# Attention products of two heads at once, in full float32, in the two column halves of TensorE

## The chip, the core and the metric

The program runs on one core of one Trainium2 chip. The metric is the device time of one execution in microseconds (us). The kernel before takes 950.82 us, the median of three runs (950.68 to 951.13). A core has a matrix engine (TensorE; PE in the rows, PEld its weight loads), VectorE (DVE), ScalarE (ACT), GpSimd (POOL), and a queue that issues transfers (SyncE; SPq). Matrix results land in eight PSUM banks. Data enters and leaves by DMA.

## The reference

Four batches of eight heads, 576 positions, head size 64; the result of the attention feeds two dense blocks.

```
scores = q @ k.T / 8 ; bias[i, j] = -(cum[i] - cum[j]), cum = cumsum(max(s, 0))
scores = where(causal, -1e9, scores + min(bias, 0))
attn   = exp(scores - rowmax) / (rowsum + 1e-9)
x      = (attn @ v)  as (2304, 512)          # the attention product of this document
x      = ((x @ w1) * (x @ w2)) @ w3 @ w_out  # 512 -> 1024 -> 1024 -> 512
h      = x @ w_in ; out = (h - tanh(h)) @ w_out2   # 512 -> 2048 -> 512
```

All inputs and the output are float32.

## The kernel before, in words

Nearly all products are made in a reduced format in three parts: an operand is split into a rounded high part and a low rest, and high x high, high x low and low x high are added up in PSUM. `copy` rounds (ScalarE or VectorE), `sub` forms the rest (VectorE or GpSimd), `split` does both. Full float32 needs no split, but each matmul then runs as two records on TensorE, of two array cycles per column each.

One head (`head`) is worked like this. Queries come in five tiles of 64 or 128 rows. For each tile the scores of all keys up to the diagonal are formed in a bank, the bias rows being part of the contraction; VectorE reads the bank, subtracts and takes the row maximum (L664), ScalarE takes the exponential and the row sum (L670). `flip` transposes the tile on TensorE (L702) into a bank, from which it is copied to SBUF. `pv` multiplies by the values: `pv(0)` for queries 0 to 319 (three key chunks, 320, 192 and 64 columns), `pv(1)` for queries 320 to 575 (five chunks, 3 x 256, 192, 64 columns), both in bank 2. After the odd head of a pair, `inverses` turns the row sums into factors: a transpose (L682), a copy, a DMA to DRAM (r_d) and one back that spreads them over partitions (xr); then the pair's output xf is multiplied (L779) and split into xh and xl, which the products with w1 and w2 (L801, six matmuls per step and 128 channels) read. Each product sums over four pairs of heads, so none ends before the fourth pair of a batch is there.

There are two kinds of head. The eight heads of batch 0 (`full`) use full float32 for scores (L651) and for `pv` (L742, 80 stationary columns: 64 of the values and 16 of padding), from buffer `en`. The other 24 heads split queries and keys (qs, kh, kl, q2; L653 and L654) and, for `pv`, the values (vs, high and low side by side: 128 stationary columns) and the transposed tile (eh, el). L746 multiplies both value halves by eh, L744 the high half by el; the two halves of the bank are then added (a copy to pvt, and L753). q2 holds the low part of the queries and, under it, rows of constants from `fix` that select the bias rows of kl; `constants` brings them by two DMAs. The buffers of odd split heads are in a pool `spl`, which opens only when the pool `nat` of batch 0 (rel, en) is closed, at head 8; `constants(1)` follows that.

While batch 0 runs, w1 and w2 are brought in and converted (`assemble`, L489 to L495, then a split), 16 pieces of 128 x 512.

The order of all instructions is made by a planner in the kernel (`Plan.order`): each operation has a price and a priority, and the planner starts on each engine what is ready, in the order of priority, by its own clock. Where its TensorE would wait before 215 us it inserts small matmuls on `msk` (L548, 128 columns, fillers), which compute nothing that is used. Fillers and order are fixed in the program: on the chip a filler runs whether there is a wait or not, and an instruction that waits holds up those behind it on its engine.

After the attention come w3 @ w_out (L861 to L863), the products with it (L899 to L901) and the second dense block (L938, L959 to L961).

Of the kernel before, what the change touches and what calls it, by code (L numbers as in the profile page):

```python
# [29 lines left out]
VW = D + 16  # L30
# [4 lines left out]
EN = 1024 + 128  # L35
# [288 lines left out]
def tile_kernel(ctx, tc, qk, v, s, w1, w2, w3t, w_out, w_in, w_out2, out):  # L324
# [113 lines left out]
    kh = [p_.buf(f"kh{i}", [P, S], F32R) for i, p_ in enumerate((att, spl))]  # L438
    kl = [p_.buf(f"kl{i}", [P, S], F32R, n=2) for i, p_ in enumerate((att, spl))]
    q2 = [p_.buf(f"q2{i}", [P, S], F32R, n=2) for i, p_ in enumerate((att, spl))]  # L440
    vs = [p_.buf(f"vs{i}", [P, 5, P], F32R, n=2) for i, p_ in enumerate((att, spl))]
# [97 lines left out]
    def constants(i):  # L539
        for a in (D, D + 5):  # L540
            dma(lambda a=a: q2[i].t[a:a + 5].bitcast(F32), lambda: fix.t[D:D + 5], 5 * S * 4, [(fix, 1)], [(q2[i], 1)], PARAM["cst"], issue=830.0)
# [18 lines left out]
    for e in e2[:1] + [en] + e2[1:]:  # L560
        if e is en:
            zero([later(en, 1024, EN, low), later(en, 0, D, low)], [P, D], [en], 30, r=scan)
# [7 lines left out]
    for V in rv:  # L570
        zero([lambda V=V: V.t[:, 5 * D:]], [VW - D], [(V, 1)], 30, r=scan)
    for x in (eh, el):
        zero([later(x, EB + 1024, ETOT, low), later(x, 0, D, low)], [P, D], [x], PARAM["kbp"] - 10, r=scan)
# [10 lines left out]
    for a, n, o, w_, ts in ((0, 2 * NH, 0, 2 * S, [0, 1, 3, 4]), (0, NH, 2 * S, S, [2])):  # L584
        v_ = lambda x, a=a, n=n, o=o, w_=w_: x.t[a:a + n, o:o + w_]
        act(lambda v_=v_: nc.scalar.activation(v_(eh), v_(rel), AF.Copy), w_, [(rel, ts)], [(eh, ts)], PARAM["kbp"])
        sub(lambda v_=v_: v_(el), lambda v_=v_: v_(rel), lambda v_=v_: v_(eh), w_, [(rel, ts), (eh, ts)], [(el, ts)], PARAM["kbp"])
    constants(0)
    for n, x in enumerate((eh, el)):
        dma(lambda n=n, x=x: kb_d.t[:, n, 0:3], lambda x=x: x.t[:NH, :3 * S].bitcast(F32).rearrange("h (t s) -> h t s", s=S), NH * 3 * S * 4, [(x, [0, 1, 2])], [kb_d], PARAM["kbp"] + 100)  # L590
        dma(lambda n=n, x=x: kb_d.t[:, n, 3:5], lambda x=x: x.t[NH:2 * NH, :2 * S].bitcast(F32).rearrange("h (t s) -> h t s", s=S), NH * 2 * S * 4, [(x, [3, 4])], [kb_d], PARAM["kbp"] + 100)
# [9 lines left out]
    def head(h, full, groups=(0, 1)):  # L601
# [6 lines left out]
        e, eb = e2[i % len(e2)], 0 if full else EB  # L608
        qa, qb = (0 if 0 in groups else 320), (S if 1 in groups else 320)
        nv = (qb + P - 1) // P  # L610
        R, RV, Q, Q2, KH, KL, V = rqk[i], rv[i], qs[i], q2[i], kh[i], kl[i], vs[i]
# [5 lines left out]
        else:  # L617
# [6 lines left out]
            P * nv * D * 4, [], [(RV, 0)], pr + PARAM["rv"], issue=520.0)  # L624
        rq, rk = (lambda: R.t[:, 0:S]), (lambda: R.t[:, S:2 * S])
        if not full:
# [6 lines left out]
            split(lambda: V.t[:, :nv, 0:D], (V, 0), lambda: V.t[:, :nv, D:], (V, 1), lambda: RV.t[:, :nv * D].rearrange("p (c d) -> p c d", d=D), nv * D + 100, [RV], p_)  # L633
# [57 lines left out]
        def flip(t):  # L691
# [4 lines left out]
            for js in [list(range(min(4, nch)))] + ([[4]] if nch > 4 else []):  # L696
# [8 lines left out]
                if js == [4]:  # L705
                    n, nq = 1, P - D
                    view = lambda d: d.t[:D, eb + 1024 + D:eb + 1024 + P]
                    src = lambda bk=bk: bk.t[:D, D:P]
                else:
                    o = q0 if t < 3 else eb + q0 - 320  # L710
# [6 lines left out]
                if full:  # L717
                    copy(lambda view=view: view(en), src, n * nq, [bk], [(en, [t] if t < 3 else [[0, 1, 3], [2, 4]][t - 3])], p_, psum=True)
                else:
                    split(lambda view=view: view(eh), (eh, t), lambda view=view: view(el), (el, t), src, n * nq, [bk], p_, psum=True)  # L720

        def pv(grp):
            p_ = pr + PARAM["pv"]
            bk = pv_ring.next()
            if grp == 0:
                q0, n, parts = 0, 320, [0, 1, 2]
                lst = [(0, 0, 320, P), (1, 384, 192, P), (2, 768, 64, P)]
            else:
                q0, n, parts = 320, 256, [3, 4]
                lst = [(c, eb + c * 256, 256, P) for c in range(3)] + [(3, eb + 832, 192, P), (4, eb + 1088, 64, P)]  # L730
            X = xf[(h // 2) % 2]
            o = (h % 2) * D
            if full:
                seq = [(x, 0) for x in lst]
            else:
                seq = [(x, 0) for x in lst[:-2]] + [(lst[-1], 0), (lst[-1], 1)] + [(x, 1) for x in lst[:-2]] + [(lst[-2], 0), (lst[-2], 1)]

            def mm():
                for j, ((c, a, w_, kk), low) in enumerate(seq):
                    go = dict(start=j == 0, stop=j == len(seq) - 1, skip_group_check=True)  # L740
                    if full:
                        nc.tensor.matmul(bk.t[:VW, n - w_:n], RV.t[:kk, c * D:c * D + VW], en.t[:kk, a:a + w_], **go)  # L742
# [22 lines left out]
        if 0 in groups:  # L765
            pv(0)
# [246 lines left out]
```

## Time and profile before

| what | value |
| --- | --- |
| median of 3 runs | 950.82 us |
| the profiled execution, its own time | 950.12 us |
| its span, first to last instruction | 948.4 us |
| TensorE busy in the span | 936.3 us (99%) |
| VectorE, ScalarE, GpSimd busy | 686.5, 595.1, 416.5 us |
| share of TensorE in the chain that ended last | 95% |

Times inside the profile count from the start of the span. The busy time of TensorE contains the fillers, and the end of a matmul is modelled: how long a run of matmuls takes is read from the start of its first to the start of what follows. The profiled execution is 1.7 us longer than its span.

### The profile page before, as it was taken

Reading aid. Unit: us, or ns where it says so; the run is one execution under the profiler, and the core shown is the slowest. Engines: PE = TensorE matmul, PEld = TensorE weight load, DVE = VectorE, ACT = ScalarE, POOL = GpSimd, SP = SyncE. Lnnn points to the kernel's source line nnn. Section 1 sums busy time; section 2 is a strip of 40 time slices with the busy share of each in tenths; the row PEclk is TensorE's granted clock in tenths of the full one; section 3 lists DMA queues with packets and bytes.
Section 4 is the critical chain, followed back from the end, with each engine's and each line's share of the span. In section 5 each row is a group of like instructions: output and inputs, shape, how many; then the busy total and the mean of one; then the engine's idle time right before and its main releaser. Section 6 shows DMA issues by size and latency. Waiting matters only on the chain.

```text
span 948.4 us, 15455 instructions
## 1 busy us (share of the span) xinstructions
PE 936.3 (99%) x5214; PEld 822.9 (87%) x5214; DVE 686.5 (72%) x1399; ACT 595.1 (63%) x1329; POOL 416.5 (44%) x354
## 2 busy tenths in 40 slices
PE   9997999999999999999999999999999999999998
PEld 7776999999999999899888888888888888888887
DVE  8998888688786569993699669985555556645654
ACT  5887677788888544443545367766555555665565
POOL 3458766545564244323988525442222222222321
PEclk9997999999999999999999999999999999999999
DMA  5664566575542135476798532221020101000010
GB/s 185 202 203 139 171 186 203 149 240 152 153 145 76 54 109 189 164 237 210 230 373 297 206 133 88 79 100 45 1 88 1 45 1 45 22 23 1 1 46 23
DMA packets 64309, 118.97 MB, mean 125 GB/s; under 512 B 6435, under 2 KB 34323, under 8 KB 64230
## 3 DMA queue, kind: packets, MB, share of 16 engines
q1 hardware_dynamic: 64230, 117.99, 38.4%
q8 instruction: 41, 0.67, 0.3%
q14 instruction: 38, 0.31, 0.1%
HBM read 88.81 MB, written 25.46 MB: 120 GB/s over the span
## 4 chain that ended last, share of the span: by engine, by line
PE 95%; DVE 3%; ACT 1%; issue 1%; DMA 0%; POOL 0%; SPq 0%; DVEq 0%
PE bank L801 21%; PE bank L938 21%; PE bank L961 7%; PE bank L959 7%; PE bank L960 7%; PE bank L702 5%; PE bank L901 3%; PE bank L899 3%; PE bank L900 3%; PE bank L744 2%; PE bank L654 2%; PE bank L653 2%; PE bank L746 2%; PE bank L861 2%; PE bank L651 2%; PE bank L863 2%
## 5 line engine op out<-in xcount | busy, mean ns | idle before, releaser
L393 POOL TENSOR_TENSOR gl<-pg,gh 128x512 fp32r<-128x512 f32 (+1 forms) x78 | 99.9, 1280 | 254.5 <-ACT gh L387 247.7
L938 PE MATMUL bank<-x2b,wih 128*128 128x512 f32 (+1 forms) x640 | 182.6, 370 | 0.0
L938 PEld LDWEIGHTS bank<-x2b,wih 128*128 128x128 f32 x640 | 116.9, 188 | 22.1
L938 PE MATMUL bank<-x2b,wil 128*128 128x512 f32 (+1 forms) x320 | 117.9, 369 | 0.0
L949 DVE TENSOR_TENSOR pg<-bank,u 128x512 f32<-128x512 f32 (+1 forms) x80 | 50.4, 630 | 90.4 <-POOL gl L393 86.3
L961 PE MATMUL bank<-voh,gl 128*128 128x512 f32 x288 | 112.9, 392 | 0.0
L959 PE MATMUL bank<-voh,gh 128*128 128x512 f32 x288 | 112.8, 392 | 0.0
L960 PE MATMUL bank<-vol,gh 128*128 128x512 f32 x288 | 112.7, 391 | 0.0
L670 ACT ACTIVATE e<-e,nmx 128x320 f32<-128x320 f32 (+4 forms) x160 | 89.0, 558 | 37.6 <-DVE nmx L664 36.6
L387 ACT ACTIVATE gh<-pg 128x512 fp32r<-128x512 f32 (+1 forms) x80 | 47.0, 588 | 99.2 <-PE bank L960 95.8
L952 DVE TENSOR_TENSOR th<-bank,th 128x512 f32<-128x512 f32 (+1 forms) x80 | 50.7, 634 | 45.9 <-ACT th L948 45.8
L664 DVE CUSTOM_DVE_ANT_0 e<-bank,msk 128x320 f32<-128x320 f32 (+4 forms) x160 | 65.6, 421 | 23.1 <-PE bank L654 14.5
L953 DVE COPY_PREDICATED pg<-mk,th 128x512 f32<-128x512 uint32 (+1 forms) x80 | 78.2, 978 | 2.5 <-ACT mk L951 0.9
L702 PE MATMUL bank<-ident,e 128*128 128x128 f32 (+1 forms) x480 | 75.3, 274 | 0.5 <-DVE el L391 0.5
L495 DVE SCALAR_TENSOR_TENSOR wt<-wraw,wt 128x512 uint32<-128x512 uint32 x72 | 72.5, 1007 | 0.8
L493 DVE SCALAR_TENSOR_TENSOR wt<-wraw,wt 128x512 uint32<-128x512 uint32 x72 | 71.8, 997 | 1.0
L393 POOL TENSOR_TENSOR xl<-cf,xh 128x512 fp32r<-128x512 f32 (+1 forms) x40 | 54.8, 1396 | 34.3 <-DMA cf<-c_d 23.9
L938 PEld LDWEIGHTS bank<-x2b,wil 128*128 128x128 f32 x320 | 60.3, 188 | 10.6
L801 PE MATMUL bank<-xh,w1h 128*128 128x384 f32 x192 | 68.6, 357 | 0.1
L391 DVE TENSOR_TENSOR el<-bank,eh 64x64 fp32r<-64x64 f32 (+2 forms) x144 | 62.6, 458 | 8.3 <-ACT eh L387 7.0
L801 PE MATMUL bank<-xh,w2h 128*128 128x384 f32 x192 | 67.9, 354 | 0.0
L951 ACT ACTIVATE mk<-u,const 128x512 f32<-128x512 f32 (+1 forms) x80 | 54.1, 676 | 18.8 <-DVE pg L953 18.5
(135 smaller groups left out, 2496.1 us busy)
## 6 DMA issues: line engine op xcount, KB each, us to landing
rqk<-qk SPq DMA_DIRECT2D x24, 576.0 KB
wraw<-w_out SPq DMA_DIRECT2D x24, 512.0 KB
c_d<-cst SPq DMA_DIRECT2D x48, 192.0 KB
wraw<-w SPq DMA_DIRECT2D x16, 512.0 KB
wraw<-w3t SPq DMA_DIRECT2D x16, 512.0 KB
wraw<-w_in SPq DMA_DIRECT2D x16, 512.0 KB
cf<-c_d SPq DMA_DIRECT2D x32, 256.0 KB
x_d<-x2s SPq DMA_DIRECT2D x16, 512.0 KB
```

What stands on the lines that cost most here:

```text
L393: o.append(("POOL", c_pool2(n), lambda: nc.gpsimd.tensor_tensor(dst(), a(), b().bitcast(F32), op=ALU.subtract)))
L493: dve(lambda: nc.vector.scalar_tensor_tensor(t_.t, h32(), 0xC0000000, t_.t, op0=ALU.bitwise_and, op1=ALU.bitwise_or), 512, [r_, t_], [t_], ...
L495: dve(lambda: nc.vector.scalar_tensor_tensor(t_.t, l32(), 29, t_.t, op0=ALU.logical_shift_right, op1=ALU.bitwise_or), 512, [r_, t_], [t_], ...
L664: nc.vector.tensor_tensor_reduce(e.t[:nq, EOFF[t] + k0:EOFF[t] + k1], bk.t[:nq, :k1 - k0], bi.t[:nq, bo + k0:bo + k1], -0.125, 3.0e38 if f ...
L670: act(lambda: nc.scalar.activation(et(), et(), AF.Exp, bias=nmx.t[:nq, i, tm:tm + 1], scale=-1.0, accum_out=ssum.t[:nq, pj, t, i:i + 1]), ...
L702: nc.tensor.transpose(bk.t[:rows, n * P:(n + 1) * P], e.t[:, EOFF[t] + c * P:EOFF[t] + c * P + rows], ident.t)
L801: nc.tensor.matmul(bk.t[:, :TB], w_.t[:, k, f * P:(f + 1) * P], x_.t[:, k, o:o + TB], start=k == 0 and i == 0, stop=k == KC - 1 and i == 2)
L938: nc.tensor.matmul(bk.t[:, :w], w_.t[:, k, a], X2.t[:, i, k, :w], start=k == 0 and n == 0, stop=k == KC - 1 and n == 2)
L953: dve(lambda pg=pg, mk=mk, th=th, c_=c_: nc.vector.copy_predicated(c_(pg), c_(mk).bitcast(U32), c_(th)), w, [mk, th], [pg], pr, two=True)
L959: nc.tensor.matmul(bank[n].t, gh.t[:, a], voh[f].t, start=f == 0, stop=False)
L960: nc.tensor.matmul(bank[n].t, gh.t[:, a], vol[f].t, start=False, stop=False)
L961: nc.tensor.matmul(bank[n].t, gl.t[:, a], voh[f].t, start=False, stop=f == NF2 - 1)
```

## The change

All 32 heads now use full float32 in `pv`, and one `pv` serves a pair of heads. `flip` copies the transposed tile of either head into a buffer of its own (en[0], en[1]); when the odd head of the pair is transposed, `pv` issues for each chunk a matmul of the even head into partitions 0 to 63 of the bank and one of the odd head into 64 to 127. The stationary operands are the raw values (64 columns, no padding), so each of the two uses one half of the array's columns. One copy of 128 partitions takes the result to xf. Gone are vs, eh, el, pvt, their splits and the addition L753. The score operands of odd heads (qs, kh, kl, q2) move from `spl` to the pool `att`, open from the start, and `constants` is called for both at the start. The split of the bias rows goes to a buffer kbs. There are four value buffers instead of two. The table of priorities (`PARAM`) is the same. One build option sets the SBUF scratch of dynamic DMAs.

```diff
+def f_pair(n):
+    return 2 * [(112.0, 0.8333 * n + 8.0)]
...
-    rv = [att.buf(f"rv{i}", [P, 4 * D + VW], n=2) for i in range(2)]
-    en = nat.buf("en", [P, EN], n=5)
-    spl = Pool("spl", "right")
-    qs = [p_.buf(f"qs{i}", [P, S], F32R, n=2) for i, p_ in enumerate((att, spl))]
...
-    vs = [p_.buf(f"vs{i}", [P, 5, P], F32R, n=2) for i, p_ in enumerate((att, spl))]
+    rv = [att.buf(f"rv{i}", [P, 5 * D]) for i in range(4)]
+    kbs = nat.buf("kbs", [P, 3 * S], F32R, n=10)
+    qs = [p_.buf(f"qs{i}", [P, S], F32R, n=2) for i, p_ in enumerate((att, att))]
...
-    eh = att.buf("eh", [P, ETOT], F32R, n=5)
-    el = att.buf("el", [P, ETOT], F32R, n=5)
-    pvt = att.buf("pvt", [D, 320])
+    en = [att.buf(f"en{i}", [P, ETOT], n=5) for i in range(2)]
...
-    constants(0)
...
+    for i in range(2):
+        constants(i)
...
-            split(lambda: V.t[:, :nv, 0:D], (V, 0), lambda: V.t[:, :nv, D:], (V, 1), lambda: RV.t[:, :nv * D].rearrange("p (c d) -> p c d", d=D), nv * D + 100, [RV], p_)
...
-                if full:
-                    copy(lambda view=view: view(en), src, n * nq, [bk], [(en, [t] if t < 3 else [[0, 1, 3], [2, 4]][t - 3])], p_, psum=True)
-                else:
-                    split(lambda view=view: view(eh), (eh, t), lambda view=view: view(el), (el, t), src, n * nq, [bk], p_, psum=True)
+                copy(lambda view=view: view(en[i]), src, n * nq, [bk], [(en[i], t)], p_, psum=True)
...
+            V2 = rv[2 * pj:2 * pj + 2]
...
+                for j, (c, a, w_) in enumerate(lst):
+                    for k in range(2):
+                        nc.tensor.matmul(bk.t[k * D:(k + 1) * D, n - w_:n], V2[k].t[:, c * D:(c + 1) * D], en[k].t[:, a:a + w_],
+                                         start=j == 0, stop=j == len(lst) - 1, skip_group_check=True)
+            pe([y for x in lst for y in f_pair(x[2])], mm, V2 + [(en[k], parts) for k in range(2)], [bk], p_)
+            copy(lambda: X.t[:, q0:q0 + n], lambda: bk.t[:, :n], n, [bk], [X], p_, psum=True)
...
-        if 0 in groups:
+        if 0 in groups and i:
             pv(0)
...
             nat.close()
-            pl.op([("X", 0.0, lambda: None)], w=[eh])
-            spl.open()
-            constants(1)
...
+    nc = bacc.Bacc("TRN2", target_bir_lowering=False, num_devices=1, dynamic_dma_scratch_size=1024)
```

The planner makes a new order of it. Three places. First TensorE before, the end of batch 0: `pv(1)` of head 7 (L742, rv1), `pv(0)` of head 8 (L746 and L744, vs0), and the first scores of head 9 (L653, L654 with q21, one of the two q2). A row's end gives the rows and columns of the result, and "x3" a repetition.

```order
L742 MATMUL bank2_60<-en_136,rv1_107 80x256 x3
L742 MATMUL bank2_60<-en_136,rv1_107 80x192
L742 MATMUL bank2_60<-en_136,rv1_107 80x64
L702 MATMUL bank3_61<-ident_78,e0_113 128x128 x3
L746 MATMUL bank2_60<-eh_119,vs0_112 128x320
L746 MATMUL bank2_60<-eh_119,vs0_112 128x64
L744 MATMUL bank2_60<-el_120,vs0_112 64x64
L744 MATMUL bank2_60<-el_120,vs0_112 64x320
L746 MATMUL bank2_60<-eh_119,vs0_112 128x192
L744 MATMUL bank2_60<-el_120,vs0_112 64x192
L653 MATMUL bank1_59<-kh1_989,qs1_988 64x64
L654 MATMUL bank1_59<-kl1_990,q21_991 64x64
```

TensorE with the change, `pv(1)` of heads 6 and 7, and the next product (L782, formerly L801):

```order
L730 MATMUL bank2_60<-en0_124,rv2_108 64x256
L730 MATMUL bank2_60<-en1_125,rv3_109 64x256
L730 MATMUL bank2_60<-en0_124,rv2_108 64x256
L730 MATMUL bank2_60<-en1_125,rv3_109 64x256
L730 MATMUL bank2_60<-en0_124,rv2_108 64x256
L730 MATMUL bank2_60<-en1_125,rv3_109 64x256
L730 MATMUL bank2_60<-en0_124,rv2_108 64x192
L730 MATMUL bank2_60<-en1_125,rv3_109 64x192
L730 MATMUL bank2_60<-en0_124,rv2_108 64x64
L730 MATMUL bank2_60<-en1_125,rv3_109 64x64
L782 MATMUL bank6_64<-xh_89,w1h_94 128x384
```

Each chunk now stands twice, once with the even head's en0 and rv2 and once with the odd head's en1 and rv3, where before one head's chunks followed each other; of the split products none is left.

Second the queue of DMA issues, before, at the same time of the program: the constants of q21 (`fix`) are behind the loads of heads 9 to 11.

```order
L384 DMA rqk0_103<-qk 128x2x320
L384 DMA rv0_106<-v 128x192
L384 DMA kl1_990<-kb_d_68 10x320
L384 DMA q21_991<-fix_102 5x576
L384 DMA rv1_107<-v 128x192
L384 DMA q21_991<-qs1_988 64x320
L384 DMA rqk1_104<-qk 128x2x320
L384 DMA q21_991<-fix_102 5x576
L384 DMA rv1_107<-v 128x192
L384 DMA kl1_990<-kb_d_68 10x320
```

With the change, at the start of the program:

```order
L386 DMA q20_116<-fix_102 5x576
L386 DMA rqk1_104<-rel_139 3x1x576
L386 DMA rqk0_103<-rel_139 2x1x576
L386 DMA kb_d_68<-kbs_140 32x1728
L386 DMA q20_116<-fix_102 5x576
L386 DMA rqk1_104<-rel_139 2x1x576
L386 DMA q21_117<-fix_102 5x576 x2
L386 DMA kb_d_68<-kbs_140 32x1152
L386 DMA wraw1_81<-w2 128x1024
L386 DMA wraw3_105<-w1 128x1024
```

The constants of q21 (here q21_117) have moved from rows 77 and 81 of this queue's order to row 17, ahead of the second weight piece (wraw1).

Third TensorE with the change, at the scores of head 9 (L649 and L650, formerly L653 and L654): the same place of the work as the last rows of before in the first pair. L698 transposes (formerly L702), L546 is a filler (formerly L548), of a load and a matmul each.

```order
L649 MATMUL bank1_59<-kh1_113,qs1_111 64x64
L650 MATMUL bank1_59<-kl1_115,q21_117 64x64
L649 MATMUL bank0_58<-kh1_113,qs1_111 128x192
L650 MATMUL bank0_58<-kl1_115,q21_117 128x192
L698 MATMUL bank5_63<-ident_78,e0_118 128x128 x2
L546 LDWEIGHTS msk_101
L546 MATMUL bank2_60<-msk_101 128x128
L649 MATMUL bank1_59<-kh1_113,qs1_111 128x320
L650 MATMUL bank1_59<-kl1_115,q21_117 128x320
L698 MATMUL bank3_61<-ident_78,e0_118 128x128 x3
L546 LDWEIGHTS msk_101
L546 MATMUL bank2_60<-msk_101 128x128
```

Here fillers stand between scores and transposes. From the fourth `inverses` transpose to the first product that reads the fourth pair there were 2, and there are 131. In the whole program there are 370 fillers, 164 before; the 206 more all stand before that product. In counts of instructions: VectorE 1401 before and 1202 now, ScalarE 1171 and 1109, GpSimd 356 and 325, DMA issues 443 both.

## Rows read from the trace of the kernel before

**Rows 1.** The page, parts 1, 2 and 4: shares, slices of 23.7 us.

```profile
PE 936.3 (99%) x5214; PEld 822.9 (87%) x5214; DVE 686.5 (72%) x1399; ACT 595.1 (63%) x1329; POOL 416.5 (44%) x354
...
PEclk9997999999999999999999999999999999999999
...
PE 95%; DVE 3%; ACT 1%; issue 1%; DMA 0%; POOL 0%; SPq 0%; DVEq 0%
```

**Rows 2.** Busy us: stretch, PE, PEld, DVE, ACT, POOL; then PEclk, DMA share, GB/s.

```profile
200.00:300.00 100.00, 99.54 (x733) 97.74 (x732) 76.70 (x245) 83.68 (x242) 55.67 (x48) 1.00 0.49 146
```

**Rows 3.** The same for stretches of 10 us up to 100.

```profile
0.00:10.00 10.00, 8.94 (x112) 8.25 (x113) 7.88 (x33) 2.16 (x6) 4.47 (x11) 1.00 0.56 158
...
60.00:70.00 10.00, 10.00 (x61) 7.86 (x61) 9.77 (x29) 9.22 (x26) 5.11 (x5) 1.00 0.61 196
...
80.00:90.00 10.00, 4.58 (x21) 3.97 (x22) 9.91 (x18) 5.67 (x16) 9.13 (x10) 0.64 0.46 124
90.00:100.00 10.00, 10.00 (x61) 9.62 (x61) 7.06 (x26) 7.46 (x25) 5.03 (x5) 0.85 0.52 150
```

**Rows 4.** The chain of waits, 0 to 130 us: start, length, what.

```profile
16.55 0.99 PE bank L742 x6
...
21.19 1.75 PE bank L742 x10
...
24.03 0.56 PE bank L548 x10
```

**Rows 5.** TensorE in order of time, 240 to 246 us: two split head groups.

```profile
240.27 0.55 PE L746 MATMUL bank<-eh,vs 128*128 128x256 f32 x4
...
241.27 0.49 PE L702 MATMUL bank<-ident,e 128*128 128x128 f32 x3
...
245.16 0.34 PE L746 MATMUL bank<-eh,vs 128*128 128x320 f32 x2
...
245.74 0.27 PE L702 MATMUL bank<-ident,e 128*64 128x128 f32 x1
```

**Rows 6.** TensorE in order of time, 73 to 89 us.

```profile
73.01 0.27 PE L653 MATMUL bank<-kh,qs 128*64 128x64 f32 x1
...
73.54 0.27 PE L682 MATMUL bank<-ident,ssum 128*10 128x128 f32 x1
...
74.06 0.60 PE L702 MATMUL bank<-ident,e 128*128 128x128 f32 x4
...
79.29 0.50 PE L702 MATMUL bank<-ident,e 128*128 128x128 f32 x3
81.26 0.41 PE L746 MATMUL bank<-eh,vs 128*128 128x320 f32 x2 [1.46 <-DVE eh L388]
...
82.19 0.19 PE L653 MATMUL bank<-kh,qs 128*64 128x64 f32 x1
86.39 0.29 PE L654 MATMUL bank<-kl,q 74*64 74x64 f32 x1 [4.01 <-DMA q<-fix]
...
88.22 0.67 PE L801 MATMUL bank<-xh,w1h 128*128 128x384 f32 x1
```

**Rows 7.** The DMA queue's issues, 80 to 84 us.

```profile
80.37 0.79 SPq L384 DMA_DIRECT2D q<-fix  x1
...
83.00 0.75 SPq L384 DMA_DIRECT2D q<-fix  x1
```

**Rows 8.** GpSimd in order of time, 82 to 87 us.

```profile
82.27 1.72 POOL L779 TENSOR_TENSOR xf<-xf,xr 128x64 f32<-128x64 f32 x2
...
84.95 1.85 POOL L393 TENSOR_TENSOR xl<-xf,xh 128x576 fp32r<-128x576 f32 x1
```

**Rows 9.** VectorE groups by line and form.

```profile
L391 DVE TENSOR_TENSOR el<-bank,eh 128x512 fp32r<-128x512 f32 x48 | 31.9, 682 | 1.9 <-ACT eh L387 1.5
```

**Rows 10.** Weight loads by line and form.

```profile
L746 PEld LDWEIGHTS bank<-eh,vs 128*128 128x128 f32 x192 | 31.1, 189 | 2.2 <-POOL w1l L393 1.7
...
L744 PEld LDWEIGHTS bank<-el,vs 128*64 128x64 f32 x192 | 19.9, 136 | 0.2 <-DVE el L391 0.2
```

More of the change, by code (lines that the diff above doesn't have):

```diff
@@ L559, in tile_kernel @@
     low = slice(D, P)
-    for e in e2[:1] + [en] + e2[1:]:
-        if e is en:
-            zero([later(en, 1024, EN, low), later(en, 0, D, low)], [P, D], [en], 30, r=scan)
+    for e in e2[:1] + [None] + e2[1:]:
+        if e is None:
+            for x in en:
+                zero([later(x, EB + 1024, ETOT, low), later(x, 0, D, low)], [P, D], [x], 30, r=scan)
             zero([lambda: ssum.t], [20], [ssum], -5, 1.0)
@@ L569, in tile_kernel @@
             zero([later(e, EOFF[0], EOFF[0] + D, low)], [D], [(e, 0)], -10 if e is e2[0] else 92, r=scan)
[L570 to L573, printed above, removed]
     zero([lambda: const.t[:, 0:1]], [1], [const], 5.0e4, SQ_B, r=scan)
@@ L607, in head @@
         n_head[0] += 1
-        e, eb = e2[i % len(e2)], 0 if full else EB
+        e = e2[i % len(e2)]
         qa, qb = (0 if 0 in groups else 320), (S if 1 in groups else 320)
         nv = (qb + P - 1) // P
-        R, RV, Q, Q2, KH, KL, V = rqk[i], rv[i], qs[i], q2[i], kh[i], kl[i], vs[i]
+        R, RV, Q, Q2, KH, KL = rqk[i], rv[2 * pj + i], qs[i], q2[i], kh[i], kl[i]
         rows = D if full else P
@@ L726, in pv @@
                 q0, n, parts = 0, 320, [0, 1, 2]
-                lst = [(0, 0, 320, P), (1, 384, 192, P), (2, 768, 64, P)]
+                lst = [(0, 0, 320), (1, 384, 192), (2, 768, 64)]
             else:
                 q0, n, parts = 320, 256, [3, 4]
-                lst = [(c, eb + c * 256, 256, P) for c in range(3)] + [(3, eb + 832, 192, P), (4, eb + 1088, 64, P)]
+                lst = [(c, EB + c * 256, 256) for c in range(3)] + [(3, EB + 832, 192), (4, EB + 1088, 64)]
             X = xf[(h // 2) % 2]
-            o = (h % 2) * D
@@ L733, in pv @@
[L733 to L736, printed above, removed]
-            def mm():
[L739 to L742, printed above, removed]
-                    elif low:
-                        nc.tensor.matmul(bk.t[:D, n - w_:n], V.t[:kk, c, 0:D], el.t[:kk, a:a + w_], **go)
-                    else:
-                        nc.tensor.matmul(bk.t[:, n - w_:n], V.t[:kk, c, :], eh.t[:kk, a:a + w_], **go)
@@ L747, in pv @@
-            if full:
-                pe([y for (x, _) in seq for y in f_mm4(x[2])], mm, [RV, (en, parts if grp == 0 else range(5))], [bk], p_)
-                copy(lambda: X.t[o:o + D, q0:q0 + n], lambda: bk.t[:D, :n], n, [bk], [(X, h % 2)], p_, psum=True)
-            else:
-                pe([y for (x, low) in seq for y in f_mm(x[2], D if low else P)], mm, [V, (eh, parts), (el, parts)], [bk], p_)
-                copy(lambda: pvt.t[:, :n], lambda: bk.t[D:, :n], n + 300, [bk], [pvt], p_, psum=True)
-                dve(lambda: nc.vector.tensor_tensor(X.t[o:o + D, q0:q0 + n], bk.t[:D, :n], pvt.t[:, :n], op=ALU.add), n, [bk, pvt], [(X, h % 2)], p_, extra=150.0)
+            V2 = rv[2 * pj:2 * pj + 2]
@@ L771, in head @@
                 flip(t)
-            pv(1)
+            if i:
+                pv(1)
         if h % 2:
@@ L835, in tile_kernel @@
         if b == B - 1:
-            spl.close()
             att.close()
```

32 lines of the change are left out of this document (15 added, 17 removed).

## The prediction

> **What bounds the kernel now.** I read the page first. TensorE is busy for 936.3 of 948.4 us and carries 95% of the chain that ended last [rows 1]. A busy figure so near the span says little, since fillers count as work, so I went on to the stretches. From 200 to 300 us TensorE is full (99.54 of 100) while VectorE has 76.70 and GpSimd 55.67 [rows 2]; the clock row shows full clock in all slices but one [rows 1]. After about 100 us the time is thus the sum of what TensorE is given, and relieving another engine is worth nothing there. The first 100 us are different: TensorE shares the bound with VectorE and ScalarE (9.77 and 9.22 of 10 us from 60 to 70), and from 80 to 90 us it is busy for 4.58 of 10 only, at a mean granted clock of 0.64, then at 0.85 from 90 to 100 [rows 3]. So I price three things: the TensorE work of the value products, the fillers, and the hole at 80 us.
>
> **The value products.** In batch 0 a head's two runs of L742 take 0.99 and 1.75 us, 2.74 together, the order being tight there [rows 4]; eight heads 21.9 us. In a split head `pv(1)` runs from 240.27 to 241.27 and `pv(0)` from 245.16 to 245.74, each up to the next transpose [rows 5]: 1.58 us, 24 heads 37.9 us. Before, the value products cost 59.8 us.
>
> With the change a pair has the columns of one L742 head twice, once in each half of the array. No row of before shows two column halves at work together; this is the unknown of the case. Bounds: if the halves run fully side by side, a pair costs what one head did, 2.74 us, 16 pairs 43.8 us, a saving of 16.0. If one waits for the other, it costs 5.48 us, 16 pairs 87.7 us, a loss of 27.9. I take them as side by side, since the two halves share no weights and no result rows, but not perfectly. Each full-precision matmul is two records, and the two of one half must follow each other. In program order the first record of a group has no partner yet, nor has the last. That exposes at most one record per group: 320 of the 1152 columns that `pv(0)` streams (two passes over 576), 0.28 us, and 256 of 2048 in `pv(1)`, 0.22 us. So a pair costs 2.74 to 3.24 us. I take 3.1, in the upper half: 49.6 us, a saving of 10.2.
>
> The Trainium skill, "TensorE: Matmul & The Clock Gate", section "Part 3: Packing small matmuls", says that matmuls in different column tiles run at once, each further tile adding about 4 ns. By it a pair is some 2.8 us (an estimate from that page and L742) and the result some 5 us lower than mine; no run here shows it yet.
>
> **The fillers.** There are 206 more. A run of ten takes 0.56 us [rows 4], 56 ns each: 11.5 us. They run whether needed or not. They stand where the order expects TensorE to wait for the softmax and the weight conversion, and the rows support that: in batch 0 the others are nearly full [rows 3] and the change takes little from them there, eight copies of a result to xf. About 9.5 us of value products leave batch 0 (8 heads at 2.74 less 4 pairs at 3.1), and fillers take their place. This is the part of the gain that I expect not to see.
>
> **The hole at 80 us.** TensorE waits 1.46 us for a split (eh, on VectorE) and then 4.01 us for the constants of q2 [rows 6], whose two transfers are issued only at 80.37 and 83.00 us [rows 7], because odd heads' operands cannot exist before `nat` is closed. Behind that wait in TensorE's queue stand the scores of heads 9 and 10 and then all products. 5.5 us are lost by waiting. Granted clocks of 0.64 and 0.85 mean that the lower of the two levels, 1.2 instead of 2.4 GHz, held for 7.2 of the first 10 us and 3.0 of the next, so from about 82.8 to 93.0 us. TensorE works in it from 86.39 on, 6.6 us at half speed, 3.3 us lost. Together 8.8 us.
>
> With the change the constants come in the first 20 us, and eh is gone. What is late next is the fourth pair: its inverses' transpose is at 73.54 us [rows 6], its output is multiplied from 82.27 and the low part xl ends at 84.95 + 1.85 = 86.80 us [rows 8]: 13.3 us after. So even without the constants no product of that pair could have started before 86.80, against 88.22 in the trace [rows 6]. In the new order, between the same two points, TensorE has 131 fillers (7.3 us), one `pv(1)` and one `pv(0)` (3.1 us), the first three score tiles of three heads (1.0 us each, 73.01 to 74.06 less the small transpose in it [rows 6]), six products of 384 steps and 19 transposes of 256 steps (1.0 and 2.1 us at the 0.43 ns that L742 takes per step, 0.99 us for 2,304), 16.5 us in all. That is longer than 13.3, so I expect the pair to be ready when TensorE gets there, with 3 us to spare. TensorE also reaches the transpose some 4 to 5 us earlier: the value products ahead of it shrink by about 9 us, and 77 of the added fillers (4.3 us) stand there. The fillers also keep the engine from standing still. From 0 to 10 us, where it mainly ran fillers, the granted clock was 1.00 [rows 3], so I take the upper level here and count the 3.3 us as won.
>
> A new order brings waits that its planner did not foresee; the old one had 5.5 us of them here. I add 2.0 us, with 0 and 6 as ends.
>
> **What costs and gives nothing.** VectorE loses 144 subtractions like L391 (682 ns for the largest form [rows 9]) and 48 additions L753, and GpSimd 32 splits of values. All but the first heads' lie after 100 us, beside a full TensorE. If TensorE became so short of work there that VectorE set the pace, it would be seen as idle time; at 76.70 of 100 us, falling, this is far off. The copy of a pair's result covers 128 partitions instead of 64, with the same columns. The second weight piece is issued behind eight more transfers, at up to 0.79 us each [rows 7] 6 us later at most; VectorE has softmax to do in that time, and if it falls behind by this, that is the third rival below.
>
> **The sum.** 948.4 - 10.2 + 11.5 - 8.8 + 2.0 = 942.9 us of span. The profiled execution was 1.7 us longer than its span, and 0.7 below the median of the runs: 945 us.
>
> **The rivals.**
> *The halves take turns.* One stream of columns enters the array at a time, and the second half waits. For it: nothing in the trace shows an overlap of two streams, and L742 with 80 of 128 columns is a single stream. Against it: the two use separate columns and partitions. A pair costs 5.48 instead of 3.1 us, 16 pairs 38 us more, and since the order is fixed nothing absorbs it: 983 us. The change turns slower from 3.1 + 5.8/16, about 3.5 us per pair, on: there the gain of 5.8 us is gone.
> *The weight loads come into the open.* A pair has 32 loads of 64 columns. Loads take 136 ns with 64 columns and 189 with 128 [rows 10], so 64 columns occupy some 53 ns of the load path. If half of the 32 cannot hide beside the other half's stream, 16 pairs pay 13.6 us: 959 us; if all, 972. Against it: in before loads hide behind streams (L744 waited 0.2 us in 192 loads).
> The Trainium skill, "TensorE: Matmul & The Clock Gate", in the same section, states that a load overlaps matmuls in flight only where the row group differs, and both halves use all rows. The trace disagrees for one tile after another, and shows nothing for two halves.
> *The hole stays.* The fourth pair, or the softmax of heads 8 and 9, comes later than the order assumes, TensorE stands still behind it, the clock falls again, and the fillers have run all the same. For it: VectorE had 9.91 of 10 us there [rows 3]. Against it: the 3 us to spare, and less work on VectorE. Then the 8.8 us are not won: 952 us, with the small value of unforeseen waits.
>
> **Chances.** My forecast 0.68, with its own range of 937 to 951 us (2.74 to 3.24 us per pair, 0 to 6 us of new waits); turns 0.12; loads 0.08; hole 0.12. The range that leaves out no more than 2 in 10 reaches over the hole and the cheaper half of the loads, 937 to 960 us; the turns are left out. A measurement of this kernel tells some 0.2% (1.9 us) from no change. Faster than 948.9 us: 0.64 of the forecast's 0.68 and 0.03 of the hole, 0.67. Within: 0.04, 0.07 of the hole and 0.01 of the loads, 0.12. Slower than 952.7: the turns 0.12, loads 0.07, hole 0.02, 0.21.
>
> **What would show it.** In the changed profile the start of a run of L730 to the start of what follows gives the price of a pair: 2.7 to 3.2 us for both groups if the halves overlap, 5.5 if they take turns, 3.9 to 4.8 if loads show, and then the weight loads of L730 have waits of their own. The clock row should have no low slice near 90 us, no wait on q2's constants should be left, and the first dense run of products should start 2 to 4 us earlier than 88.22. The filler group should count 370. After 100 us TensorE should be as full as before, with VectorE lower. I am wrong if TensorE has more idle time before 100 us than the 8.8 us that I take away, if a pair costs over 3.5 us, or if the dense part after 330 us, which the change doesn't touch, changes its length.

## The result: 5.5 us slower, most of it lost before 96 us

The changed kernel takes 956.47 us in the median (955.67 to 957.1, four runs), the kernel before 950.98 beside it: a ratio of 1.0056, 95% interval 1.0039 to 1.0074. The forecast was 945.0 and faster. The profiled execution took 956.8 us with a span of 955.1.

### The profile page after: what moved, and what is told of

Its sections match the earlier page's. It is cut to its first block, busy times and chain, and to the rows that moved or that the text cites. A ratio compares the mean times of both kernels' runs of the same rounds, so it can differ in the third digit from the quotient of the medians.

```text
span 955.1 us, 15454 instructions
## 1 busy us (share of the span) xinstructions
PE 942.2 (99%) x5420; PEld 810.9 (85%) x5420; DVE 611.6 (64%) x1200; ACT 568.8 (60%) x1267; POOL 393.4 (41%) x323
## 4 chain that ended last, share of the span: by engine, by line
PE 95%; DVE 3%; ACT 1%; issue 1%; ACTq 0%; DVEq 0%
PE bank L915 21%; PE bank L782 20%; PE bank L938 7%; PE bank L936 7%; PE bank L937 7%; PE bank L698 5%; PE bank L730 5%; PE bank L876 3%; PE bank L877 3%; PE bank L878 3%; PE bank L546 2%; PE bank L647 2%; PE bank L649 2%; PE bank L650 2%; PE bank L838 2%; PE bank L840 2%
## 5 line engine op out<-in xcount | busy, mean ns | idle before, releaser
L936 PE MATMUL bank<-voh,gh 128*128 128x512 f32 x288 | 112.8, 392 | 0.0
L698 PE MATMUL bank<-ident,e 128*128 128x128 f32 (+1 forms) x480 | 77.0, 276 | 1.7 <-ACT e L666 0.9
L389 ACT ACTIVATE en<-bank 64x64 f32<-64x64 f32 (+3 forms) x166 | 64.3, 407 | 16.9 <-PE bank L698 15.2
L491 DVE SCALAR_TENSOR_TENSOR wt<-wraw,wt 128x512 uint32<-128x512 uint32 x72 | 73.1, 1016 | 1.2
L789 DVE TENSOR_TENSOR cst<-bank,asb 128x384 f32<-128x384 f32 x48 | 26.6, 554 | 68.9 <-PE bank L782 52.4
L782 PE MATMUL bank<-xh,w1h 128*128 128x384 f32 x192 | 69.2, 361 | 0.1
L782 PE MATMUL bank<-xh,w2h 128*128 128x384 f32 x192 | 68.3, 356 | 0.0
```

The source lines that it names most:

```text
L389: pl.op([("ACT", c_act(n, psum), lambda: nc.scalar.activation(dst(), src(), AF.Copy)), ("DVE", c_dve(n, not psum), lambda: nc.vector.tenso ...
L491: dve(lambda: nc.vector.scalar_tensor_tensor(t_.t, h32(), 0xC0000000, t_.t, op0=ALU.bitwise_and, op1=ALU.bitwise_or), 512, [r_, t_], [t_], ...
L698: nc.tensor.transpose(bk.t[:rows, n * P:(n + 1) * P], e.t[:, EOFF[t] + c * P:EOFF[t] + c * P + rows], ident.t)
L782: nc.tensor.matmul(bk.t[:, :TB], w_.t[:, k, f * P:(f + 1) * P], x_.t[:, k, o:o + TB], start=k == 0 and i == 0, stop=k == KC - 1 and i == 2)
L936: nc.tensor.matmul(bank[n].t, gh.t[:, a], voh[f].t, start=f == 0, stop=False)
```

## The profile after

The page of the changed kernel, parts 1 and 2, against [rows 1]:

```profile
PE 942.2 (99%) x5420; PEld 810.9 (85%) x5420; DVE 611.6 (64%) x1200; ACT 568.8 (60%) x1267; POOL 393.4 (41%) x323
...
PEclk9999999999999999999999999999999999999999
```

VectorE lost 75 us of work and TensorE gained 6. Busy time of stretches of the changed kernel (PE, PEld, DVE, ACT, POOL; then PEclk), against [rows 2, 3]:

```profile
80.00:90.00 10.00, 7.15 (x87) 6.75 (x86) 7.76 (x18) 5.35 (x19) 5.37 (x6) 0.90 0.54 169
90.00:100.00 10.00, 9.97 (x92) 8.68 (x91) 6.81 (x17) 5.75 (x20) 6.20 (x7) 0.93 0.35 103
...
200.00:300.00 100.00, 99.95 (x742) 90.28 (x741) 43.95 (x175) 79.28 (x236) 47.02 (x38) 1.00 0.46 142
```

The hole at 80 us is shallower and its clock higher (0.90 against 0.64), but no engine is busy for even 8 of its 10 us, where in [rows 3] VectorE had 9.91: the engines wait for one another. TensorE of the changed kernel in order of time, from the last value products of batch 0 to the first product that reads the fourth pair:

```profile
70.39 1.20 PE L730 MATMUL bank<-en,rv 128*64 128x320 f32 x12
71.85 0.66 PE L698 MATMUL bank<-ident,e 128*128 128x128 f32 x4 [0.26 <-ACT e L666]
...
74.28 0.27 PE L678 MATMUL bank<-ident,ssum 128*10 128x128 f32 x1 [1.39 <-DVE ssum L677]
...
75.59 1.96 PE L730 MATMUL bank<-en,rv 128*64 128x256 f32 x20
77.47 0.44 PE L782 MATMUL bank<-xh,w1h 128*128 128x384 f32 x1
...
87.16 0.27 PE L678 MATMUL bank<-ident,ssum 128*6 128x128 f32 x1 [2.85 <-DVE ssum L677]
...
90.22 1.74 PE L730 MATMUL bank<-en,rv 128*64 128x320 f32 x12
...
95.58 0.42 PE L782 MATMUL bank<-xh,w1h 128*128 128x384 f32 x1
```

The wait for q2's constants is gone, as forecast. In its place stand two waits for the reciprocals of the row sums, at the fourth and the fifth `inverses` transpose (L678), and the dense products start at 95.58 us, not 88.22 [rows 6]. From there to the last matmul it is 855.5 us, 856.2 before. So on balance the loss lies before 96 us. It isn't quite all of it: the new order does more ahead of that product (twelve more transposes, and the fifth pair's `pv(0)` for both its heads), so the rest should be shorter by more than 0.7; but from 100 to 200 us TensorE is busy for 98.2 us, where before it had all 100.

Summed over the trace up to that product, each TensorE instruction counted from its start to the next one's, so that a wait counts for the instruction before it, in us (the last two columns are experiments told below, without the addition L676 in the same order and in a new one):

| | before | after | without the addition | new order |
|---|---|---|---|---|
| fillers | 11.64 | 29.18 | 23.88 | 21.71 |
| value products | 22.93 | 14.55 | 14.02 | 13.64 |
| transposes | 16.90 | 18.12 | 17.80 | 16.69 |
| full scores | 25.35 | 26.54 | 26.53 | 26.20 |
| split scores | 6.90 | 2.64 | 4.05 | 3.17 |
| first products | 3.43 | 3.49 | 3.49 | 3.75 |
| sum | 87.16 | 94.51 | 89.78 | 85.16 |

What VectorE did ahead of the two transposes:

```profile
71.83 2.15 DVE L676 TENSOR_SCALAR ssum<-ssum 128x10 f32<-128x10 f32 x1
74.01 0.22 DVE L677 RECIPROCAL ssum<-ssum 128x10 f32<-128x10 f32 x1
...
83.66 3.13 DVE L676 TENSOR_SCALAR ssum<-ssum 128x6 f32<-128x6 f32 x1 [0.34 <-ACT e L666]
86.82 0.19 DVE L677 RECIPROCAL ssum<-ssum 128x6 f32<-128x6 f32 x1
```

L676 adds 1e-9 to ten or six numbers per partition. Undisturbed it takes 0.16 us; here 2.15 and 3.13. GpSimd of the changed kernel in the same time:

```profile
71.53 1.05 POOL L395 TENSOR_TENSOR kl<-rqk,kh 64x320 fp32r<-64x320 f32 x1
72.55 1.39 POOL L395 TENSOR_TENSOR xl<-xf,xh 128x576 fp32r<-128x576 f32 x1
...
83.11 0.93 POOL L395 TENSOR_TENSOR kl<-rqk,kh 64x320 fp32r<-64x320 f32 x1
84.01 0.32 POOL L760 TENSOR_TENSOR xf<-xf,xr 128x64 f32<-128x64 f32 x1
84.28 1.26 POOL L395 TENSOR_TENSOR w2l<-wt,w2h 128x512 fp32r<-128x512 f32 x1
85.50 1.26 POOL L760 TENSOR_TENSOR xf<-xf,xr 128x512 f32<-128x512 f32 x1
...
93.65 1.71 POOL L395 TENSOR_TENSOR xl<-xf,xh 128x576 fp32r<-128x576 f32 x1 [4.21 <-ACT en L389]
```

GpSimd's runs end at 72.55 + 1.39 = 73.94 and 85.50 + 1.26 = 86.76 us; the additions end at 73.98 and 86.79. So the first waited through two GpSimd instructions, the second through four. That is not the rule. Of the twenty additions in this kernel ten took over 0.25 us; all ten started while GpSimd worked, and eight of them ended with the one GpSimd instruction that they met, three of these although GpSimd's next followed at once, as here:

```profile
123.96 1.43 POOL L395 TENSOR_TENSOR kl<-rqk,kh 64x576 fp32r<-64x576 f32 x1 [0.52 <-DVE kh L390]
124.17 1.25 DVE L676 TENSOR_SCALAR ssum<-ssum 128x6 f32<-128x6 f32 x1
125.35 1.00 POOL L760 TENSOR_TENSOR xf<-xf,xr 128x64 f32<-128x64 f32 x2
```

Why the two on the path waited through more stays open. After that ScalarE's queue loses more:

```profile
87.47 0.27 ACT L389 ACTIVATE rinv<-bank 6x128 f32<-6x128 f32 x1 [3.46 <-PE bank L678]
...
92.04 0.44 ACT L389 ACTIVATE xf<-bank 128x320 f32<-128x320 f32 x1 [2.01 <-PE bank L730]
92.49 0.35 ACT L666 ACTIVATE e<-e,nmx 64x64 f32<-64x64 f32 x1
...
92.84 0.67 ACT L389 ACTIVATE xh<-xf 128x576 fp32r<-128x576 f32 x1
```

The fourth pair's output was multiplied by 86.76, but its rounding to xh stands in the order behind the copy of the next pair's result (xf), which waits for `pv(0)` at 90.22 on TensorE, which stands behind the held transpose at 87.16. So xh starts at 92.84 and xl ends at 95.36. TensorE itself shows no wait after 87.16: the fifth pair's `pv(0)`, head 10's scores and transposes and 61 fillers (4.4 us) stand ahead of the products in its order, and it comes to them at 95.58.

## The experiments

Theory A: the addition, held by GpSimd's runs, makes the fourth and fifth transposes late, and the fixed order turns that into the loss. B: VectorE and ScalarE are short of time as such. C: the added fillers hold TensorE up. Each time below is a median, given beside the kernel before, run on the same chip: 951.0 to 951.2 us in all three sets.

**Without the addition, same order.**

```
-dve(lambda: nc.vector.tensor_scalar(sv(), sv(), 1.0e-9, None, op0=ALU.add), n, [], [(ssum, ks)], ...)
+dve(lambda: None, n, [], [(ssum, ks)], ...)
```

> The changed kernel in its own order, but the addition of 1e-9 to the row sums (L676) issues nothing; a sum is at least 1, so that nothing else changes. Theory A (the small addition is held by GpSimd's runs, 2.15 us ahead of the fourth inverses transpose and 3.13 us ahead of the fifth, and the fixed order passes it on to the products at 95.58 us): the fourth L678 comes near 72.3 instead of 74.28 us, the fifth 3 to 5 us earlier than 87.16, the dense products at 91 to 93, 952 to 954 us in all. Theory B (VectorE's and ScalarE's work as such is late, the addition only waits where others would): the reciprocal or the next instruction waits as long, 956 to 957 us. Theory C (the added fillers hold TensorE up): within 1 us of 956.5.

950.96 us, ratio 0.9992 (0.9984 to 1.0001): 5.5 us less than with the addition, somewhat more than expected. TensorE, then VectorE:

```profile
72.72 0.27 PE L678 MATMUL bank<-ident,ssum 128*10 128x128 f32 x1
...
82.88 0.27 PE L678 MATMUL bank<-ident,ssum 128*6 128x128 f32 x1
...
90.84 0.42 PE L782 MATMUL bank<-xh,w1h 128*128 128x384 f32 x1
```

```profile
82.40 0.19 DVE L677 RECIPROCAL ssum<-ssum 128x6 f32<-128x6 f32 x1 [0.33 <-ACT e L666]
82.51 3.34 DVE L488 TENSOR_SCALAR wt<-wt 128x512 f32<-128x512 f32 x1
...
87.50 0.21 DVE L660 CUSTOM_DVE_ANT_0 e<-bank,msk 64x64 f32<-64x64 f32 x1
```

A holds: the transposes come 1.6 and 4.3 us earlier, the products 4.7, and after the products another 1.1 us of the span are gone. The same GpSimd run now holds the next instruction of that kind, a weight conversion (L488, 0.42 us when free), and behind it head 10's scores; that is left over.

**The kernel before without the addition, same order.** The same edit there.

> The kernel before with the same addition issuing nothing, in its own order. Theory A: there the addition ahead of the fourth and the fifth inverses transpose took 0.16 us and only the one at 41.09 us was held, by 0.8 us: 950 to 951 us, no change that can be measured; the gain of the edit belongs to the new order. If the addition is dear everywhere (after 96 us it is held by up to 1.6 us ten times): 945 to 948 us.

949.53 us, ratio 0.9981 (0.9973 to 0.9990): 1.5 us. A small gain, not none, just outside what A expected; the edit is worth 5.5 in the new order and 1.5 in the old.

**Without the last 146 fillers, same order.**

```
-        nc.tensor.matmul(bank[2].t[:, :P], x, x, start=True, stop=True)
+        if n_[0] <= 224: nc.tensor.matmul(bank[2].t[:, :P], x, x, start=True, stop=True)
```

> The changed kernel in its own order, of the 370 fillers only the first 224 (those up to the third inverses transpose); the other 146, 14 us from start to start, issue nothing. Theory A: they stand where TensorE would wait anyway, so TensorE is idle instead, the dense products start within 1.5 us of 95.58, and 955 to 958 us; if the granted clock falls in the idle time as it did at 80 us in the kernel before (0.64), up to 3 us more, 960. Theory C (the fillers are in the way of ready work): 8 to 14 us of them go, the dense products start at 84 to 88, 945 to 950 us.

957.56 us, ratio 1.0063 (1.0049 to 1.0077); the dense products start at 95.49. Taking these 146 out gains nothing, so C is out as far as they go; the first 224 stayed in. TensorE is idle where fillers were, and its clock falls:

```profile
80.00:90.00 10.00, 5.24 (x28) 3.28 (x27) 8.54 (x22) 4.93 (x20) 4.74 (x6) 0.77 0.57 174
```

The lower clock costs time too, so what a filler costs by itself is not shown by this.

**Each pair's value products head by head.**

```
-for j, (c, a, w_) in enumerate(lst):
-    for k in range(2):
+for k in range(2):
+    for j, (c, a, w_) in enumerate(lst):
```

> The changed kernel, each pair's value products issued as all of one head (one column half), then all of the other, in place of one from each in turn. If two halves overlap only because their instructions alternate: a pair costs about 5.4 us instead of 3.1, of which batch 0 hides a part, 985 to 993 us. If alternation is not what makes it (each instruction takes what it takes): a pair stays at 3.1 us and 956 to 957 us.

984.94 us, ratio 1.0355 (1.0338 to 1.0373). TensorE at the fourth pair, to be set against 70.39 and 75.59 above:

```profile
75.33 1.79 PE L730 MATMUL bank<-en,rv 128*64 128x320 f32 x12
77.05 0.66 PE L698 MATMUL bank<-ident,e 128*128 128x128 f32 x4
...
80.53 3.30 PE L730 MATMUL bank<-en,rv 128*64 128x256 f32 x20
```

The same instructions take 4.95 us per pair from start to start over all 16, against 3.10 in turn: 29.6 us, the difference of the times 28.5. Two halves overlap where their instructions alternate; head by head little of it is left (5.48 would be two L742 heads one after the other).

**The odd heads' constants late again.**

```
-for i in range(2):
-    constants(i)
+constants(0)
...
         nat.close()
+        constants(1, [stack["right"]])
```

> The changed kernel with one step undone: the constants of the odd heads' q2 are fetched only once nat is closed, as in the kernel before; the order is made anew. If the early constants are worth what I gave them (8.8 us of hole): 962 to 966 us. Theory A (GpSimd's hold on small VectorE work and the queue behind it decide when the fourth pair is ready, the constants come in time either way or within its shadow): 955 to 959 us, the dense products again between 94 and 98 us.

970.95 us, ratio 1.0211 (1.0191 to 1.0231), but this doesn't price the constants. In the order made anew they are not as late as in the kernel before: their two transfers are issued at 58.35 us, not at 80.37 and 83.00 [rows 7], and TensorE never waits for them.

```profile
58.35 1.50 SPq L386 DMA_DIRECT2D q<-fix  x2
```

This order starts the dense products at 90.8, 4.8 us earlier than the changed kernel, and loses 12.8 us in waits far behind, at w3's products (in total, how many, the longest):

```profile
PE bank L876 <- ACT xh L389: 7.1, 1, 7.1
PE bank L877 <- POOL xl L395: 5.7, 4, 4.1
```

Neither theory foresaw that. What the early constants are worth by themselves stays open.

**Without the addition and without the last 146 fillers, same order.** The two edits together.

> The run without the addition once more (950.96 us, dense products at 90.84, 3.24 us of waits before them), and without the 146 fillers after the third inverses transpose (about 8.2 us at 56 ns). If these fillers are what TensorE spends its saved time on needlessly: dense products at 83 to 87 us, 943 to 947 us in all. If VectorE, ScalarE and GpSimd set the time of the fourth pair and of the softmax of heads 8 to 10: the waits grow by what the fillers took, dense products at 90 to 91.5, 950 to 952 us (up to 3 us more where the granted clock falls).

951.03 us, ratio 0.9997 (0.9984 to 1.0009); dense products at 90.46 against 90.84 with the fillers. So here, too, the time that the value products give back becomes filler or idle time, whichever one chooses. It agrees with this that TensorE is not the bound before 90 us, but it isn't shown: the clock fell with the idle time (0.66), and that costs time as well; `pv(0)` of the fifth pair took 2.83 us there by its row, 1.20 with the fillers:

```profile
80.00:90.00 10.00, 8.18 (x36) 5.02 (x34) 7.14 (x22) 7.04 (x23) 7.32 (x7) 0.66 0.63 171
```

**Without the addition, the order made anew.** The line of the addition is taken out, so that the planner doesn't see it.

> The changed kernel without the addition, the order made anew (332 fillers instead of 370; other queues move with it). Theory A, on what is left of the loss after the addition is gone (a conversion L488 held 3.34 us by GpSimd ahead of head 10's scores at 82.51, and xh of the fourth pair behind that head's exponentials on ScalarE): a new order doesn't know of these holds either, 947 to 952 us. If the added fillers or the old order's place of xh were the rest: 943 to 946 us.

944.98 us, ratio 0.9933 (0.9921 to 0.9946). ScalarE, GpSimd and TensorE at the fourth pair:

```profile
84.56 0.68 ACT L389 ACTIVATE xh<-xf 128x576 fp32r<-128x576 f32 x1
```

```profile
85.31 1.42 POOL L395 TENSOR_TENSOR xl<-xf,xh 128x576 fp32r<-128x576 f32 x1 [3.01 <-ACT xh L389]
```

```profile
85.92 0.55 PE L697 MATMUL bank<-ident,e 128*128 128x128 f32 x3
86.22 0.42 PE L781 MATMUL bank<-xh,w1h 128*128 128x384 f32 x1
```

Here xh stands ahead of the next pair's copy, GpSimd rests from 82.3 to 85.31 while VectorE converts weights unheld, and the dense products start at 86.22. My expectation by A was too timid: the order has no knowledge of holds, but it met few. Which of the moved instructions did it was not tried one by one. That the time meets the forecast of 945.0 is luck: it is another kernel, in another order.

**And the subtractions on VectorE.** The planner's prices are changed besides, so that it gives the splits' subtractions to VectorE: `dsub0` 979.7 to 0, `dsub` 5134.3 to 600, `pool` -71.7 to 300, `spp` 349.6 to 500, `dcopy0` 29.4 to 10, `dother0` 1000 to 300, `act` -76.1 to -40, `fl` 112.8 to 100, `early` 154617 to 200000.

> As the run with the new order and no addition, and the planner's prices are changed so that the splits' subtractions go to VectorE and hardly any to GpSimd (84 GpSimd rows instead of 328, 1423 VectorE rows instead of 1170). Theory A: with GpSimd's runs gone the VectorE instructions that they held take their undisturbed times (L488 0.42 us, L491 0.69), which is more than the 0.4 to 0.7 us that each subtraction adds to VectorE: dense products at 83 to 88 us, 942 to 948 us. Theory B (VectorE's own work is the bound of the first 90 us): the added subtractions, some 20 there, lengthen it by 10 us: dense products at 96 to 102, 955 to 965 us.

943.76 us, ratio 0.9918 (0.9904 to 0.9932), the fastest of all, 0.8% below the kernel before; dense products at 85.60. From 200 to 300 us VectorE has more to do than in the changed kernel (56.20 against 43.95 us), GpSimd a third of what it had, and TensorE is full:

```profile
200.00:300.00 100.00, 100.00 (x739) 91.49 (x736) 56.20 (x185) 76.23 (x225) 16.15 (x14) 1.00 0.40 122
```

**The kernel before without the addition, the order made anew.**

> The kernel before without the addition, the order made anew: what the change itself is worth once neither kernel has the addition and each has its own order, to be set against 944.98 us of the changed kernel so treated. Theory A: in the kernel before the addition cost 1.5 us in its old order, and a new order of this kernel moves no limit: 948 to 952 us; the change is then worth 3 to 7 us. If a new order helps any kernel as much as it helped the changed one (6 us beyond the addition): 942 to 946 us, and the change is worth nothing.

954.84 us, ratio 1.0037 (1.0024 to 1.0051): slower than in its old order (949.53), outside both expectations. Its first dense run starts at 93.28, and the constants' wait is there:

```profile
PE bank L654 <- DMA q<-fix: 2.6, 1, 2.6
```

So making the order anew moves either kernel by 5 to 6 us, the one up and the other down, and a single order doesn't tell the worth of the change.

**The addition with GpSimd quiet, and the same order without it.** The prices of the run at 943.76, once with the addition and once with it issuing nothing.

> The changed kernel with the addition in it, and the subtractions of the splits on VectorE (87 GpSimd rows instead of 325): the order is made anew with those prices. To be compared with the next run, which has the same order without the addition. Theory A (GpSimd's runs hold the addition): with GpSimd nearly silent the additions take 0.15 to 0.3 us, and the two runs differ by less than 1.5 us (in the old order the addition cost 5.5). If the addition is dear by itself: again 4 to 6 us apart.

> As the run before it in the same order, the addition issuing nothing. Theory A: within 1.5 us of it, both at 944 to 950 us (the planner of this order still reserves time for the addition, so that it is not the order of the run at 943.76). If the addition is dear by itself: 4 to 6 us faster than the run before it.

949.97 us (ratio 0.9987, 0.9975 to 0.9998) with it, 950.20 (0.9993, 0.9981 to 1.0005) without. The addition's twenty instances (duration min, median, max in ns), first in the changed kernel, then in the quiet one:

```profile
L676 DVE TENSOR_SCALAR ssum<-ssum x20: 156/222/3130, 24.1 to 300.2; 128x10 f32<-128x10 f32 x12, 128x6 f32<-128x6 f32 x4, 128x4 f32<-128x4 f32 x4
```

```profile
L676 DVE TENSOR_SCALAR ssum<-ssum x20: 153/162/1119, 23.8 to 294.8; 128x10 f32<-128x10 f32 x12, 128x6 f32<-128x6 f32 x4, 128x4 f32<-128x4 f32 x4
```

In this order the addition costs nothing that can be told from the scatter of the runs (948.8 to 952.5 us with it, 948.5 to 953.5 without). The order is a new one as well, so the two times alone don't speak for GpSimd; the durations do: the longest is 1.12 us here, under one of the few GpSimd instructions left, and 3.13 there. Together with the run without the addition and the ends of the held additions this is what A rests on. The order weighs much here, too: the run at 943.76 has the same prices and no addition either, and 950.20 is 6.4 us more.

**The kernel before with the subtractions on VectorE.** The addition taken out, the same prices.

> The kernel before without the addition and with the subtractions on VectorE (1614 VectorE rows instead of 1373, 126 of GpSimd instead of 359): what the same repair does without the change. Theory A: VectorE has 76.70 us of work in each 100 there, and 15 more don't fit beside what it must do in time; TensorE waits for it and the time is 960 to 985 us: the repair is open only because the change takes 144 subtractions and 48 additions from VectorE. If GpSimd's holds are what VectorE suffers from in the kernel before too: 944 to 950 us.

972.97 us, ratio 1.0229 (1.0213 to 1.0245). That is inside A's range, but the trace doesn't show A's mechanism. VectorE has 92 of the first 100 us, yet so it has in the run at 943.76 (92.61), and the first dense run starts at 88.77, only 0.55 later than in the kernel before. The loss lies behind it. TensorE is idle for 13.9 of the 160 us from 340 to 500, where VectorE has 126.94 us of work; the kernel before has 129.28 there:

```profile
340.00:500.00 160.00, 146.08 (x718) 130.39 (x717) 126.94 (x212) 70.64 (x124) 31.35 (x21) 0.95 0.58 185
```

The largest waits are for the rounding of splits, on ScalarE:

```profile
PE bank L800 <- ACT xh L387: 7.6, 2, 4.6
...
PE bank L898 <- ACT xh L387: 6.8, 1, 6.8
```

The second stands at w3's products, as in the run with late constants. The prices were sought for the changed kernel, so this is no best order of the old one. That the repair needs the VectorE time that the change sets free is therefore not shown.

## Why the prediction was wrong

*The value products: right.* 3.1 us per pair and 49.6 us in all were forecast; L730 takes 49.6 from start to start. The rival of halves in turn is out: 3.10 us alternating, 4.95 head by head. So is the rival of open weight loads, which would have shown as 3.9 to 4.8. What makes the 0.36 us over one head's 2.74 was not tried. The estimate of some 2.8 us by the Trainium skill ("TensorE: Matmul & The Clock Gate", "Part 3: Packing small matmuls") was 0.3 too low, and its rule on loads by row groups, in the same section, did not bind here: a pair's 32 loads of 137 ns, 4.4 us in all, went into its 3.10 us.

*The fillers: right in size, wrong as a cost.* 370 run; up to the dense products they take 12.2 us more than before without the addition (11.5 forecast), 17.5 with it, since the waits and low clock behind them are counted there. But taking 146 out moves the dense products by no more than 0.4 us in either order, and saves nothing. I summed them as work where TensorE was not the bound; the sum came out because they fill what the value products leave.

*The hole: here it failed.* With the value products and the fillers as forecast the span would stand at 949.7 us. The hole and the new waits together were to take 6.8 us off it; they put 5.4 on (955.1), and without the addition they take 0.5 off (949.2). Two sentences on the hole were wrong. "TensorE also reaches the transpose some 4 to 5 us earlier": it came at 74.28 against 73.54 [rows 6], 0.7 later. Up to there the value products shrank by 8.2 us and the fillers grew by 6.2, but eight more transposes of softmax tiles stand ahead of it (119 against 111, with their waits 2.1 us), the full scores took 1.2 more, and the addition was held. I counted what was removed and added, not what was moved ahead. "I expect the pair to be ready when TensorE gets there, with 3 us to spare": I carried the 13.3 us of [rows 6, 8] over as if they were fixed. It took 21.1 us (74.28 to 95.36); without the addition 17.9, in the order made anew 14.7. In the kernel before, the additions of the fourth and fifth pair met a silent GpSimd (0.16 and 0.15 us) by luck of the order. One at 41.09 us took 0.96, one at 224.57 took 1.74: the sign was in the trace, and I read only the group's place, not its longest member. VectorE's 9.91 of 10 us from 80 to 90 [rows 3] were in part such waiting as well; by their undisturbed times, 0.69 and 0.42 us, these two conversions of weights alone hold 2.4 us of it (kernel before):

```profile
82.63 1.91 DVE L493 SCALAR_TENSOR_TENSOR wt<-wraw,wt 128x512 uint32<-128x512 uint32 x1
...
85.46 1.62 DVE L490 TENSOR_SCALAR wt<-wt 128x512 f32<-128x512 f32 x1
```

*The unforeseen waits: mis-sized.* 2.0 us, 0 to 6, was set for them. All twenty additions and what they drag along are 5.5 by the run without them, of which the two ahead of the fourth and fifth transpose are the larger part: the products came 4.7 earlier. Another 6 went with the order (950.96 to 944.98).

*The rival that came true* is "the hole stays", with a chance of 0.12 and 952 us. It named the late softmax of heads 8 and 9 and an engine standing still; the clock fell again, if less (0.90 and 0.93). Its price was 4.5 us low, since I had it lose the gain and not bring a new wait.

*After 100 us* the forecast holds: 99.95 of 100 us from 200 on. From 100 to 200 TensorE was idle for 1.8 us, which I had not expected.

*The signs of being wrong* that I had named did not show: before 100 us TensorE was idle for 7.3 us, a pair cost 3.10, and the second dense block kept its length. Idle time was the wrong sign, since fillers count as work and stand where TensorE waits; the start of the first dense run, 95.58 instead of 2 to 4 us before 88.22, was the right one.

In the order made anew and without the addition the change does give 944.98 us, but that is not the kernel that I predicted. Against the better of the two orders of the kernel before without the addition (949.53) it is 4.5 us less, or 0.5%. But orders alone move either kernel by 5 to 6 us, and few were tried: without the addition four of the changed kernel, from 943.76 to 950.96 us, and three of the kernel before, from 949.53 to 972.97. What the change is worth by itself stays open. Of the 11.5 us between its own order and 944.98 the addition explains 5.5; which moves of the new order gave the other 6 is not shown.

The hold is described by the Trainium skill, "SBUF — State Buffer", section "SBUF: two separate sides": a GpSimd instruction, and a VectorE instruction in a two-port mode or with two inputs in SBUF, take a shared pair of ports by an exclusive lock, and the second to come blocks for the whole instruction of the first. The traces agree as to the block: eight of the ten held additions ended with the one GpSimd instruction that they met. The two on the path waited through two and four in a row (2.15 us from 71.83, 3.13 us from 83.66). In which mode an addition runs, no trace shows.

## What to carry to other kernels

When a fixed order moves, a short instruction on the path may meet another engine's run that it missed before, so look at the longest member of its group in the old trace, not at the mean. Where TensorE is not the bound, work taken from it comes back as filler or idle time; price such a stretch by the chain that ends last. Before a change is judged, give both sides several fresh orders: here a new order alone moved the time by 5 to 6 us, up or down.

## What the hardware showed that I had not expected

In the changed kernel VectorE's forms fall in two kinds by whether GpSimd is at work when they start (mean ns with GpSimd at work, and without): L676 820 and 166, L488 1304 and 417, L491 (two inputs from SBUF) 1563 and 687; but the reciprocal of the same numbers 195 and 205, and the copy of a PSUM bank to `en` 461 and 498 (of mixed sizes), with no wait to be seen. In one pair of orders, moving work from GpSimd to the already busier VectorE cost nothing (943.76 us against 944.98; the intervals overlap, so that a gain isn't shown). And the two matmuls of a chunk, one in each column half, start 6 or 7 ns apart in 225 of 256 pairs of records, where they alternate in program order.
